# One accumulator for the weighted values of a head pair's row group

## The chip, the cores and the metric

The kernel runs on one core of a Trainium2 chip. The metric is device time in microseconds (us), the median of 3 runs: 1600.85 us before the change (1600.73 to 1602.08).

## The reference

Top-32 attention followed by a gated feed-forward layer, in float32:

```python
# q, k, v: batch 8, heads 8, sequence 576, head dim 64
scores = scale * np.matmul(q, k.transpose(0, 1, 3, 2))
kth = np.partition(scores, -32, axis=-1)[..., -32:-31]
scores = np.where(scores >= kth, scores, -1e9)
attn = np.exp(scores - np.max(scores, axis=-1, keepdims=True))
attn = attn / (np.sum(attn, axis=-1, keepdims=True) + 1e-09)
attn_out = np.matmul(attn, v)
# x: 4608 tokens x 512
gate = 1.0 / (1.0 + np.exp(-(x @ w_gate)))
out = (gate * (x @ w_val)) @ w_out          # 512 -> 1536 -> 512
```

## The kernel before, in words

Attention goes by steps. A step is one row tile `i` (128 queries; the fifth, `i == 4`, has the remaining 64) of one pair of heads `p` (four pairs) of one batch. The steps are sorted by row groups: the list `groups` holds (batch, first tile, end). Batch 0 has the groups 0-1, 2-3 and 4; odd batches have 0-1 and 2-4; even batches have 0-2 and 3-4. Within a group all row tiles of one pair come first, then those of the next pair.

For a step, `scores` forms the products of queries and keys (L191) and ScalarE (ACT) copies them out; `select` finds the threshold of each row, mostly on VectorE (DVE: L256, L260, L284) with ACT and GpSimd (POOL) beside it (L268, L274); `masked` applies the mask (DVE, L210) and spreads each row's inverse sum over a tile `inv` (POOL, L216).

Two steps later `turn` transposes the masked tile on TensorE (PE, L296, L301), three or four 128-column pieces to one PSUM tile of the ring `ps_t`, which has two tiles, and ACT copies each to `et` (L297). A buffer `et` takes the transposes of two full row tiles (256 columns), or of one (128), or of the last (64).

Then `weigh` runs once for each `et`, 108 times in all. Both heads of a pair stand in one product's 128 output rows, head A in the lower 64 and head B in the upper 64. Keys come in chunks of 128; each head has four chunks of its own, whose values fill only half of PE's columns. Their products are the half-column products (L315 for the upper half, L316 for the lower; a pair of them runs side by side). The fifth chunk is shared by the heads and is a full product, the mixed one (L317). In a 64-column block all chunks are half-column products (L320, L321), and the last two use only 64 rows of PE (L322, L323). Behind them the inverses are transposed into the other half of the same PSUM tile (L326), ACT copies these to `rs` (L329), DVE multiplies (L332, L336), and each piece is split into a rounded and a remaining part, `xh` (ACT, L339) and `xl` (POOL, L340), which the feed-forward layer reads.

`ffn` works on units of 256 or 384 tokens: the two first products as three partial products each (L368 to L370), the gate on ACT, DVE and POOL, the last product likewise (L387 to L389). Its steps are mixed among the attention's steps by the table `MILES`. During the first attention steps `split_weights` reads the weights and splits each in two parts: DVE writes a `lead` and a `frac` tile (L133 to L138), PE forms the rest from them (L140 to L142), ACT copies it out (L143).

The order of instructions on each engine is not that of the source: a scheduler sets it from data dependences, buffers and priorities. Each engine runs its own order strictly.

## Time and profile before

| | before |
|---|---|
| median of 3 runs | 1600.85 us |
| profiled execution | 1602.43 us |
| its span, first to last instruction | 1600.5 us |
| granted TensorE clock, mean | 0.988 |
| PE busy | 1534.2 us |
| DVE busy | 1317.3 us |
| ACT busy | 1127.3 us |
| POOL busy | 1097.4 us |

The profiled execution took 1.9 us more than its span. "PEld" is the weight loads of PE, which overlap its products. A busy share is a mean over the span. The ends of products on PE are modelled, so that their durations overlap: the time that PE takes for one is read from its start to the next start.

### The profile page before, as it was taken

To read this page: it belongs to the slowest core of one execution; us is meant where nothing else is said; L and a number is where in the kernel's file an instruction comes from. 1 tells how busy PE (TensorE), PEld (TensorE's weight loads), DVE (VectorE), ACT (ScalarE), POOL (GpSimd) and SP (SyncE) were. 2 spreads that over 40 slices of the span, in tenths; PEclk is the share of its full clock that TensorE was granted. 3 is DMA by queue.
4 is the path that set the end of the run, shared out by engine and by line. 5 is a ranking of instruction groups with operands and counts; after the bars stand their busy time and mean duration, and the time that the engine had idled before them with its cause. 6 is when DMAs were issued, how large, how long until landed. Compare 5 with 4: busy or idle time off the path is not lost.

```text
span 1600.5 us, 34265 instructions
## 1 busy us (share of the span) xinstructions
PE 1534.2 (96%) x10586; PEld 1397.7 (87%) x10586; DVE 1317.3 (82%) x5895; ACT 1127.3 (70%) x2531; POOL 1097.4 (69%) x1799
## 2 busy tenths in 40 slices
PE   5769889999999999999999999999999999999998
PEld 3437669999989999988999999999999999999998
DVE  7999997888998878898988788888988888888201
ACT  7778876778777777778677778768777778667221
POOL 7556876688776786688767786678766887665111
PEclk8889999999999999999999999999999999999999
DMA  7664788786755665655555575566555665564574
GB/s 268 206 204 153 235 278 320 275 300 240 272 185 181 233 225 188 201 200 194 203 200 190 214 250 191 191 235 216 192 201 180 225 229 194 195 207 170 178 283 160
DMA packets 92065, 346.65 MB, mean 217 GB/s; under 512 B 10208, under 2 KB 37344, under 8 KB 63456
## 3 DMA queue, kind: packets, MB, share of 16 engines
q1 hardware_dynamic: 91872, 344.37, 61.8%
q8 instruction: 86, 1.41, 0.4%
q14 instruction: 107, 0.88, 0.2%
HBM read 316.01 MB, written 28.31 MB: 215 GB/s over the span
## 4 chain that ended last, share of the span: by engine, by line
PE 82%; DVE 10%; DMA 3%; POOL 2%; ACT 2%; issue 1%; SPq 0%; POOLq 0%; ACTq 0%; DVEq 0%
PE pz L369 12%; PE pz L370 12%; PE pz L368 12%; PE pss L191 9%; PE pt L296 6%; PE po L315 6%; PE po L387 6%; PE po L388 6%; PE po L389 6%; PE po L317 2%; DMA wraw<-in_w_dram 2%; DVE cand L256 2%; DVE e L210 2%; PE po L326 1%; DVE kths L284 1%
## 5 line engine op out<-in xcount | busy, mean ns | idle before, releaser
L274 POOL TENSOR_TENSOR u<-s,under 128x288 f32<-128x288 f32 x576 | 457.6, 816 | 116.7 <-ACT under L268 105.2
L256 DVE MAX8 cand<-s 128x8 f32<-128x72 f32 x2304 | 349.4, 219 | 60.4 <-ACT s L198 59.3
L368 PE MATMUL pz<-xh,w 128*128 128x384 f32 (+1 forms) x1184 | 393.0, 333 | 0.2 <-ACT gf L373 0.2
L369 PE MATMUL pz<-xl,w 128*128 128x384 f32 (+1 forms) x1184 | 388.3, 328 | 1.5 <-POOL xl L340 1.5
L370 PE MATMUL pz<-xh,w 128*128 128x384 f32 (+1 forms) x1184 | 388.6, 328 | 0.0
L210 DVE SCALAR_TENSOR_TENSOR e<-s,kths,e 128x576 f32<-128x576 f32 x288 | 280.3, 979 | 5.7 <-ACT e L205 5.6
L268 ACT ACTIVATE under<-s,leads 128x576 bf16<-128x576 f32 x288 | 223.0, 775 | 77.2 <-DVE leads L260 38.8
L284 DVE MAX8 kths<-u 128x8 f32<-128x584 f32 x288 | 219.2, 761 | 41.4 <-POOL u L275 40.0
L376 POOL TENSOR_TENSOR gl<-gf,gh 128x384 fp32r<-128x384 f32 (+1 forms) x156 | 153.6, 986 | 120.7 <-ACT gh L375 116.2
L205 ACT ACTIVATE e<-s,st 128x576 f32<-128x576 f32 x288 | 209.6, 772 | 28.4 <-POOL st L264 28.0
L369 PEld LDWEIGHTS pz<-xl,w 128*128 128x128 f32 x1184 | 223.4, 189 | 2.0 <-POOL xl L340 2.0
L368 PEld LDWEIGHTS pz<-xh,w 128*128 128x128 f32 x1184 | 223.1, 189 | 1.0 <-ACT gf L373 0.4
L370 PEld LDWEIGHTS pz<-xh,w 128*128 128x128 f32 x1184 | 223.1, 189 | 0.0
L191 PE MATMUL pss<-k,qh 128*128 128x288 f32 (+2 forms) x672 | 196.2, 310 | 25.1 <-ACT s L198 18.3
L198 ACT ACTIVATE s<-pss 128x576 f32<-128x576 f32 x288 | 184.9, 642 | 41.3 <-PE pss L191 37.7
L297 ACT ACTIVATE et<-pt 128x384 f32<-128x384 f32 x384 | 178.5, 488 | 37.3 <-PE pt L296 36.5
L296 PE MATMUL pt<-ident,e 128*128 128x128 f32 x1152 | 181.7, 277 | 15.1 <-DVE e L210 11.1
L388 PE MATMUL po<-gl,w 128*128 128x384 f32 (+1 forms) x592 | 194.5, 331 | 0.7 <-POOL gl L376 0.7
L389 PE MATMUL po<-gh,w 128*128 128x384 f32 (+1 forms) x592 | 192.9, 328 | 0.0
L387 PE MATMUL po<-gh,w 128*128 128x384 f32 (+1 forms) x592 | 191.4, 337 | 0.0
L191 PE MATMUL pss<-k,ql 128*128 128x288 f32 (+2 forms) x672 | 184.4, 296 | 0.0
L296 PEld LDWEIGHTS pt<-ident,e 128*128 128x128 f32 x1152 | 142.8, 142 | 30.8 <-DVE e L210 16.4
(97 smaller groups left out, 3240.0 us busy)
## 6 DMA issues: line engine op xcount, KB each, us to landing
w<-ws SPq DMA_DIRECT2D x222, 1024.0 KB, 5.0
v<-in_v_dram SPq DMA_DIRECT2D x68, 352.0 KB, 3.6
qraw<-in_q_dram SPq DMA_DIRECT2D x160, 128.0 KB, 3.3
kraw<-in_k_dram SPq DMA_DIRECT2D x64, 288.0 KB, 3.2
wraw<-in_w_dram SPq DMA_DIRECT2D x36, 512.0 KB, 4.7
ws<-w_split SPq DMA_DIRECT2D x36, 512.0 KB, 4.4
out_dram<-acc SPq DMA_DIRECT2D x40, 192.0 KB, 5.2
out_dram<-acc SPq DMA_DIRECT2D x12, 128.0 KB, 4.7
```

Of the source, the lines that this page charges most:

```text
L191: nc.tensor.matmul(ps[:, half, o : o + n], x[:, h * P : (h + 1) * P], ks[h][:, k0 : k0 + n], start=t == 0, stop=t == len(todo) - 1,)
L210: nc.vector.scalar_tensor_tensor(e[:, j], s[:, j], kth[j], e[:, j], op0=ALU.is_ge, op1=ALU.mult, accum_out=st[:, 4 + j : 5 + j])
L256: nc.vector.max(cand[:, j, 8 * g : 8 * g + 8], s[:, j, g * SEG : (g + 1) * SEG])
L274: nc.gpsimd.tensor_tensor(u[:, j, part], s[:, j, part], under[:, j, part], op=ALU.mult)
L284: nc.vector.max(kths[:, n_tiles - col - j : n_tiles - col - j + 8], u[:, j])
L296: nc.tensor.transpose(pt[:, c], ef[:, k0 : k0 + P], ident)
L368: nc.tensor.matmul(ps, wt[:, u, 0, d], xh, start=d == 0, stop=False)
L369: nc.tensor.matmul(ps, wt[:, u, 0, d], xl, start=False, stop=False)
L370: nc.tensor.matmul(ps, wt[:, u, 1, d], xh, start=False, stop=d == NP - 1)
L387: nc.tensor.matmul(ps, wt[:, e % 2, 0, f], gh, start=f == 0, stop=False)
L388: nc.tensor.matmul(ps, wt[:, e % 2, 0, f], gl, start=False, stop=False)
L389: nc.tensor.matmul(ps, wt[:, e % 2, 1, f], gh, start=False, stop=f == FG - 1)
```

## The change

`weigh` is called once for each pair and row group, with all its blocks, and forms them side by side in the columns of one PSUM tile: 68 calls in the place of 108. Of the 40 merged calls 16 have a 256- and a 64-column block, 12 a 256- and a 128-column block, 12 a 128- and a 64-column block.

The last block comes first. Where it has 128 columns its mixed product is formed before its half-column products. The half-column products of the next block are chained to the last one of the block before, and the mixed product of the first block comes at the end. All these products get a raised priority for the scheduler. Three inverses and up to 384 columns no longer fit one PSUM bank; then the inverses go to a tile `rb` of the transposes' ring. ACT copies all inverses of a call at once.

A buffer pool `spare` is opened when the weights are split. From then on every third `et` comes from it, so there are three; it also holds `rs` with 384 columns and the `inv` tiles, four in the place of three. The `frac` tiles of the split go from three to two.

```diff
-                    frac = parts.tile([P, NP * P], F32R, tag="frac", name=f"wt_frac_{idx}_{i}")
+                    frac = parts.tile([P, NP * P], F32R, tag="frac", bufs=2, name=f"wt_frac_{idx}_{i}")
...
+        pools["spare"] = ctx.enter_context(tc.tile_pool(name="late", bufs=1, reuse_waits="tile"))
...
-        inv = bi.tile([P, P], F32, tag="inv", name=f"inv_{nm}")
+        inv = (pools["spare"] if "spare" in pools else bi).tile([P, P], F32, tag="inv", bufs=4 if "spare" in pools else 3, name=f"inv_{nm}")
...
-    def weigh(et, vt, n, invs, pieces, nm):
+    def weigh(blocks, vt, pieces, nm):
+        n = sum(cols for _, cols, _ in blocks)
+        m = sum(len(invs) for _, _, invs in blocks) * P
+        po = ps_o.tile([P, 4 * P], F32, tag="o", name=f"po_{nm}")
+        rb = po[:, 4 * P - m :]
+        if n + m > 4 * P:
+            rb = ps_t.tile([P, 4, P], F32, tag="t", name=f"rb_{nm}").rearrange("p a n -> p (a n)")[:, :m]
+        mixed = vt[:, 4:6].rearrange("p a d -> p (a d)")
+        at = [sum(cols for _, cols, _ in blocks[:x]) for x in range(len(blocks))]
+        last = None
+        for x in reversed(range(len(blocks))):
+            et, cols, _ = blocks[x]
+            top = po[:, at[x] : at[x] + cols]
+            early = x > 0 and cols > REM
+            with ExitStack() as queued:
+                queued.enter_context(tc.high_priority(offset=RAISE))
+                if early:
+                    nc.tensor.matmul(top, mixed, et[:, 4, :cols], start=True, stop=False)
+                if last is not None:
+                    queued.enter_context(tc.issue_after(last.ins))
+                if cols > REM:
+                    for c in reversed(range(4)):
+                        for d, v0, e0 in ((slice(D, P), 6, 5), (slice(0, D), 0, 0)):
+                            last = nc.tensor.matmul(
+                                top[d],
+                                vt[:, v0 + c],
+                                et[:, e0 + c, :cols],
+                                start=c == 3 and not early,
+                                stop=c == 0 and early,
+                            )
+                else:
+                    for c in range(4):
+                        nc.tensor.matmul(top[:D], vt[:, c], et[:, c, :REM], start=c == 0, stop=False)
+                        nc.tensor.matmul(top[D:], vt[:, 6 + c], et[:, c, REM:P], start=c == 0, stop=False)
+                    nc.tensor.matmul(top[:D], vt[:REM, 4], et[:REM, 4, :REM], start=False, stop=True)
+                    last = nc.tensor.matmul(top[D:], vt[:REM, 10], et[:REM, 4, REM:P], start=False, stop=True)
+                if cols > REM and not early:
+                    nc.tensor.matmul(top, mixed, et[:, 4, :cols], start=False, stop=True)
+        for t, inv in enumerate(inv for _, _, invs in blocks for inv in invs):
+            nc.tensor.transpose(rb[:, t * P : (t + 1) * P], inv, ident)
...
+        nc.scalar.activation(rs[:, :m], rb, AF.Copy)
...
-                et, o, invs = b2.tile([P, 9, 2 * P], F32, tag="et", name=f"et_{nm}"), 0, []
+                pool = pools["spare"] if "spare" in pools and turns % 3 == 2 else b2
+                et, o, invs = pool.tile([P, 9, 2 * P], F32, tag="et", name=f"et_{nm}"), 0, []
+                turns += 1
...
             if len(invs) == 2 or i >= end - 1 or i == NT - 1:
+                blocks.append((et, o, invs))
+            if i == end - 1:
...
-                weigh(et, values[g, p], o, invs, pieces, nm)
+                weigh(blocks, values[g, p], pieces, nm)
+                blocks = []
```

In the pieces of the engines' orders below, line numbers are those of the version shown: after the change the half-column products are L333 (128 rows) and L342 to L345 (64-column block), the early mixed product L327, the late one L347, the transposed inverses L350, the feed-forward products L395 to L397 and L414 to L416. `po` is the accumulator, `v` the values, `pss` scores, `pz` feed-forward sums.

On PE in batch 4, pair 3, group 0-2, before: the block of row tiles 0 and 1.

```order
L368 MATMUL pz_2_1_1_13885<-xh_1_9957,w_9_13868 128x384
L315 MATMUL po_1_3_13761<-et_0_3_13614,v_3_13491 64x256
L316 MATMUL po_1_3_13761<-et_0_3_13614,v_3_13491 64x256
...
L317 MATMUL po_1_3_13761<-et_0_3_13614,v_3_13491 128x256
L326 MATMUL po_1_3_13761<-ident,inv_0_3_13422 128x128
L326 MATMUL po_1_3_13761<-ident,inv_1_3_13561 128x128
L191 MATMUL pss_4_1_0_13787<-k_1_2_11999,qh_4_1_13495 128x288
```

The block of row tile 2 follows later as a run of its own, in the same form with 128 columns. After the change, the same group:

```order
L414 MATMUL po_6_2_1_14189<-gh_2_2_13924,w_16_14063 128x384
L327 MATMUL po_2_3_13825<-et_2_3_13807,v_3_13414 128x128
L350 MATMUL rb_2_3_13826<-ident,inv_0_3_13330 128x128
...
L414 MATMUL po_6_2_1_14189<-gh_2_3_14030,w_16_14063 128x384
L333 MATMUL po_2_3_13825<-et_2_3_13807,v_3_13414 64x128 x8
L333 MATMUL po_2_3_13825<-et_0_3_13537,v_3_13414 64x256 x8
L347 MATMUL po_2_3_13825<-et_0_3_13537,v_3_13414 128x256
L193 MATMUL pss_4_1_0_13691<-k_1_2_11921,qh_4_1_13418 128x288
```

The half-column products of both blocks stand in one run, and the mixed product of the smaller block and the inverses stand ahead, among feed-forward products.

On PE at a 64-column block, batch 5, pair 2, before:

```order
L296 MATMUL pt_2_3_0_17521<-ident,e_2_3_17162 128x128
L320 MATMUL po_4_2_17417<-et_4_2_17407,v_2_17033 64x64
L321 MATMUL po_4_2_17417<-et_4_2_17407,v_2_17033 64x64
...
L322 MATMUL po_4_2_17417<-et_4_2_17407,v_2_17033 64x64
L323 MATMUL po_4_2_17417<-et_4_2_17407,v_2_17033 64x64
L326 MATMUL po_4_2_17417<-ident,inv_4_2_17205 128x128
L296 MATMUL pt_2_3_1_17526<-ident,e_2_3_17162 128x128 x3
```

After, the same row group:

```order
L342 MATMUL po_4_2_17291<-et_4_2_17281,v_2_16924 64x64
L343 MATMUL po_4_2_17291<-et_4_2_17281,v_2_16924 64x64
L350 MATMUL rb_4_2_17292<-ident,inv_2_2_16831 128x128
...
L193 MATMUL pss_0_0_1_17173<-k_0_1_17156,ql_0_0_16929 128x288
L344 MATMUL po_4_2_17291<-et_4_2_17281,v_2_16924 64x64
L345 MATMUL po_4_2_17291<-et_4_2_17281,v_2_16924 64x64
L333 MATMUL po_4_2_17291<-et_2_2_17014,v_2_16924 64x256 x8
L347 MATMUL po_4_2_17291<-et_2_2_17014,v_2_16924 128x256
```

The 64-row pair stands directly ahead of the other block's products; here other work lies between it and its own block's first eight products. In 15 of the 28 such calls the whole run is unbroken, in 12 it is split in this way.

On DVE at the end of the weights' split, before (`wt_frac` is the fraction tile, `cand` the segments' maxima of a row tile's scores):

```order
L256 MAX cand_0_0_3328<-s_0_0_3104 128x8 x7
L137 TENSOR_SCALAR wraw_1_2638<-wt_lead_1_2640 128x512
L138 SCALAR_TENSOR_TENSOR wt_frac_0_2625<-wraw_0_2622 128x512
L262 MATCH_REPLACE cand_4_3_3200<-tops_4_3_3201,cand_4_3_3200 128x64
L260 MAX tops_0_0_3329<-cand_0_0_3328 128x8
L393 SCALAR_TENSOR_TENSOR acc_1_0_1731<-po_0_2_0_2593,acc_1_0_1731 128x256
L332 TENSOR_TENSOR rs_3_3_3079<-po_3_3_3067,rs_3_3_3079 128x256
L138 SCALAR_TENSOR_TENSOR wt_frac_1_2641<-wraw_1_2638 128x512
```

After:

```order
L139 SCALAR_TENSOR_TENSOR wt_frac_0_2625<-wraw_0_2622 128x512
L258 MAX cand_1_0_3466<-s_1_0_3190 128x8 x5
L135 SCALAR_TENSOR_TENSOR wt_lead_1_2640<-wraw_1_2638,wt_lead_1_2640 128x512
L258 MAX cand_1_0_3466<-s_1_0_3190 128x8 x11
L286 MAX kths<-u_4_3_3208 128x8
L138 TENSOR_SCALAR wraw_1_2638<-wt_lead_1_2640 128x512
L420 SCALAR_TENSOR_TENSOR acc_1_1_1746<-po_0_2_1_2607,acc_1_1_1746 128x256
L139 SCALAR_TENSOR_TENSOR wt_frac_1_2641<-wraw_1_2638 128x512
```

The last fraction now stands behind the sixteen segment maxima of a further row tile and one long maximum.

## Rows read from the trace of the kernel before

**Rows 1.** The page: busy times with shares of the span; the chain's shares.

```profile
PE 1534.2 (96%) x10586; PEld 1397.7 (87%) x10586; DVE 1317.3 (82%) x5895; ACT 1127.3 (70%) x2531; POOL 1097.4 (69%) x1799
...
PE 82%; DVE 10%; DMA 3%; POOL 2%; ACT 2%; issue 1%; SPq 0%; POOLq 0%; ACTq 0%; DVEq 0%
```

**Rows 2.** Stages: from:to, length, busy us of PE, PEld, DVE, ACT, POOL; clock; DMA.

```profile
0.00:134.00 134.00, 88.46 (x366) 54.02 (x367) 121.44 (x494) 102.37 (x208) 82.93 (x127) 0.88 0.68 224
134.00:240.00 106.00, 95.70 (x614) 75.23 (x613) 104.66 (x392) 86.02 (x191) 82.64 (x115) 0.97 0.67 225
240.00:1560.00 1320.00, 1315.02 (x9413) 1234.30 (x9412) 1084.33 (x4997) 934.34 (x2125) 926.73 (x1553) 1.00 0.62 217
```

**Rows 3.** Waits of PE after 240 us: us in total, times, longest us.

```profile
PE pt L296 <- ACT et L297: 1.7, 3, 1.0
...
PE pz L368 <- ACT gf L373: 0.2, 1, 0.2
```

**Rows 4.** Timeline of PE, 256-column block: start us, us, instruction.

```profile
806.30 0.29 PE L191 MATMUL pss<-k,qh 128*128 128x288 f32 x1
806.43 0.29 PE L191 MATMUL pss<-k,ql 128*128 128x288 f32 x1
806.65 0.43 PE L315 MATMUL po<-et,v 128*64 128x256 f32 x1
...
806.92 0.38 PE L315 MATMUL po<-et,v 128*64 128x256 f32 x1
...
807.13 0.38 PE L315 MATMUL po<-et,v 128*64 128x256 f32 x1
...
808.21 0.38 PE L315 MATMUL po<-et,v 128*64 128x256 f32 x1
...
808.53 0.70 PE L317 MATMUL po<-et,v 128*128 128x256 f32 x2
809.06 0.38 PE L326 MATMUL po<-ident,inv 128*128 128x128 f32 x2
```

**Rows 5.** Timeline of PE, the end of a 64-column block.

```profile
922.73 0.22 PE L320 MATMUL po<-et,v 128*64 128x64 f32 x1
...
922.78 0.22 PE L320 MATMUL po<-et,v 128*64 128x64 f32 x1
...
922.94 0.27 PE L322 MATMUL po<-et,v 64*64 64x64 f32 x1
...
923.05 0.22 PE L322 MATMUL po<-et,v 64*64 64x64 f32 x1
...
923.21 0.33 PE L326 MATMUL po<-ident,inv 128*128 128x128 f32 x1
```

**Rows 6.** Groups by line: busy us, mean ns | idle before, its releasers.

```profile
L317 PEld LDWEIGHTS po<-et,v 128*128 128x128 f32 x152 | 22.8, 188 | 22.4 <-issue 22.4
...
L297 ACT ACTIVATE et<-pt 128x384 f32<-128x384 f32 x384 | 178.5, 488 | 37.3 <-PE pt L296 36.5
...
L256 DVE MAX8 cand<-s 128x8 f32<-128x72 f32 x2304 | 349.4, 219 | 60.4 <-ACT s L198 59.3
...
L284 DVE MAX8 kths<-u 128x8 f32<-128x584 f32 x288 | 219.2, 761 | 41.4 <-POOL u L275 40.0
...
L216 POOL COPY inv<-st 128x128 f32<-128x128 f32 x160 | 56.5, 356 | 63.7 <-DVE st L214 30.4 <-PE po L326 14.1 <-DVE tops L260 11.0
```

**Rows 7.** Timeline of DVE and PE: fractions of the weights written and read.

```profile
134.77 1.10 DVE L138 SCALAR_TENSOR_TENSOR wt_frac<-wraw 128x512 fp32r<-128x512 uint32 x1
142.86 0.67 DVE L138 SCALAR_TENSOR_TENSOR wt_frac<-wraw 128x512 fp32r<-128x512 uint32 x1
...
150.15 0.39 PE L142 MATMUL wrest<-wt_frac,plus 128*128 128x512 f32 x1
...
228.97 0.67 DVE L138 SCALAR_TENSOR_TENSOR wt_frac<-wraw 128x512 fp32r<-128x512 uint32 x1
...
232.63 0.50 PE L142 MATMUL wrest<-wt_frac,plus 128*128 128x512 f32 x1
```

More of the change, by code (lines that the diff above doesn't have):

```diff
@@ L66, in tile_topk_attention_then_gated_ffn @@
     SOON, RUSH = 8, 15
+    RAISE = 200
     HELD = 2 * (2 * FG + NE // 2)
@@ L305, in turn @@
             nc.scalar.activation(et[:REM, 4, :P], pt[:REM, 0], AF.Copy)
-    def weigh(et, vt, n, invs, pieces, nm):
-        both = ps_o.tile([P, 4 * P], F32, tag="o", name=f"po_{nm}")
-        po, rb = both[:, :n], both[:, 2 * P :]
-        if n > REM:
-            mixed = vt[:, 4:6].rearrange("p a d -> p (a d)")
-            for c in reversed(range(4)):
-                nc.tensor.matmul(po[D:], vt[:, 6 + c], et[:, 5 + c, :n], start=c == 3, stop=False)
-                nc.tensor.matmul(po[:D], vt[:, c], et[:, c, :n], start=c == 3, stop=False)
-            nc.tensor.matmul(po, mixed, et[:, 4, :n], start=False, stop=True)
-        else:
-            for c in range(4):
-                nc.tensor.matmul(po[:D], vt[:, c], et[:, c, :REM], start=c == 0, stop=False)
-                nc.tensor.matmul(po[D:], vt[:, 6 + c], et[:, c, REM:P], start=c == 0, stop=False)
-            nc.tensor.matmul(po[:D], vt[:REM, 4], et[:REM, 4, :REM], start=False, stop=True)
-            nc.tensor.matmul(po[D:], vt[:REM, 10], et[:REM, 4, REM:P], start=False, stop=True)
-        for t, inv in enumerate(invs):
-            nc.tensor.transpose(rb[:, t * P : (t + 1) * P], inv, ident)
-        rs = b1.tile([P, 2 * P], F32, tag="rs", name=f"rs_{nm}")
-        m = len(invs) * P
-        nc.scalar.activation(rs[:, :m], rb[:, :m], AF.Copy)
-        xf = rs[:, :n]
-        if n > REM:
-            nc.vector.tensor_tensor(xf, po, rs[:, :n], op=ALU.mult)
-        else:
-            for h in range(2):
-                d = slice(h * D, h * D + D)
-                nc.vector.tensor_tensor(xf[d], po[d], rs[d, h * REM : h * REM + REM], op=ALU.mult)
@@ new lines, in weigh @@
+    def weigh(blocks, vt, pieces, nm):
[38 more added lines that the diff above has]
+            nc.tensor.transpose(rb[:, t * P : (t + 1) * P], inv, ident)
+        if "spare" in pools:
+            rs = pools["spare"].tile([P, 3 * P], F32, tag="rs", name=f"rs_{nm}")
+        else:
+            rs = b1.tile([P, 2 * P], F32, tag="rs", name=f"rs_{nm}")
+        nc.scalar.activation(rs[:, :m], rb, AF.Copy)
+        xf = rs[:, :n]
+        for (_, cols, _), o in zip(blocks, at):
+            if cols > REM:
+                nc.vector.tensor_tensor(xf[:, o : o + cols], po[:, o : o + cols], rs[:, o : o + cols], op=ALU.mult)
+            else:
+                for h in range(2):
+                    d, r = slice(h * D, h * D + D), o + h * REM
+                    nc.vector.tensor_tensor(xf[d, o : o + cols], po[d, o : o + cols], rs[d, r : r + cols], op=ALU.mult)
@@ L436, in run @@
         todo, work, at, col, ready = [], 0, 0, 0, 0
-        parts, done = {}, {}
+        parts, done, blocks, turns = {}, {}, [], 0
         taken, lead = 0, 2 * (FG + NE // 2)
@@ L499, in run @@
             if len(invs) == 2 or i >= end - 1 or i == NT - 1:
-                t, left, pieces = b * S + (i + 1 - len(invs)) * P, o, []
+                blocks.append((et, o, invs))
+            if i == end - 1:
+                t, left, pieces = b * S + first * P, sum(cols for _, cols, _ in blocks), []
                 while left:
```

## The prediction

> **What bounds the kernel now.** I read the page first, its busy shares and its chain of waits [rows 1]: TensorE (PE) is busy for 96% of the span and carries 82% of the chain. Then the busy times by stage [rows 2], because that share is a mean over two unlike stretches. Up to 240 us PE is busy 88.46 of 134 us and 95.70 of 106 us, while VectorE (DVE) has 104.66 of the second 106: there DVE sets the pace and PE has 55.8 us idle. From 240 to 1560 us PE is busy 1315.02 of 1320 us. In that stretch the end moves with PE's own work, microsecond for microsecond. Third, what PE waits for after 240 us [rows 3]: its six rows come to 5.2 us, the first of them, 1.7 us, for transposes that want a PSUM tile back from ScalarE (ACT). None of the six is a wait for a DVE mask. So what the change can give must come out of PE's instructions themselves, and the view for that is the timeline of one run of half-column products [rows 4].
>
> A busy PE hides small losses, because a product's end is modelled and overlaps the next start. They are seen between starts. In [rows 4] a 288-column score product is followed by the next 0.13 us later (806.30 to 806.43), but by the first half-column pair 0.22 us later: 0.09 us lost. From the first pair to the second are 0.27 us, between later ones 0.21: 0.05 us more. From the last pair to the mixed product are 0.32 us, 0.10 over a pair. The mixed product runs as two passes; its two and the step to the next operation take 0.53 us where two passes at a pair's rate take 0.43: 0.10 us. The weight loads say so too: the mixed product's loads sat behind 22.4 us of "issue" idle in all [rows 6], waiting for nothing but PE's own state. A 64-column block [rows 5] pays 0.10 us where it goes from its 128-row chunks to its 64-row pair (0.16 between starts, where chunks follow at 0.05 to 0.06), and 0.05 us at its end (0.16 where the pairs follow at 0.11).
>
> **The change, part by part.** The arithmetic stays: the same products, transposes and weight loads, in the same shapes. What goes is borders. Counted over the whole PE order, runs of half-column products begin 122 times before and 83 times after (108 and 68 calls, the rest are runs that other work splits), so there are 39 fewer. The sum on PE:
> - beginnings: 39 x (0.09 + 0.05) = 5.5 us less;
> - ends in 128-row half columns: 90 before, 78 after, 12 x 0.10 = 1.2 us less;
> - ends in a 64-row pair: 32 before, 5 after, 27 x 0.05 = 1.3 us less;
> - the step from 128-row chunks to the pair: 30 before, 20 after (the new order often leaves the pair for later, the second order piece shows it), 1.0 us less;
> - mixed products right behind a run: 71 and 64, 0.7 us less;
> - new: 28 steps from the 64-row pair back to 128-row half columns of another block. No row shows one. From below, a pair's end costs 0.05; from above, beginning a run and its slow first pair cost 0.14. I take 0.10, the price of the opposite step [rows 5]: 2.8 us more (1.4 to 3.9).
>
> That makes 7.0 us less on PE (5.8 to 8.3), nearly all of it after 240 us, because batch 0 merges nothing. The twelve mixed products that now come early stand among full-array work and should cost their two passes and no border.
>
> The Trainium skill, page "TensorEngine Tiling (Array Packing)", section "Tiling Modes", Key Properties, says that changing the tiling mode drains TensorE and that changing only the tile does not. The trace agrees: 0.09 to 0.10 us at changes of mode, none between the two blocks' pairs of one mode. The rule speaks against a part of this change: a 64-column block's pair is a mode of its own, so merging it with a full block adds a change. By the rule alone there are 274 changes before and 214 after, 60 x 0.10 = 6.0 us less.
>
> *The split of the weights (up to 240 us).* The fraction tile goes from three buffers to two, and the first instruction that moves for it is a DVE one. Before, DVE writes a fraction at 134.77 us which PE reads at 150.15, and writes the one two later at 142.86 [rows 7]. With two buffers that write has to come after the read. The order puts it 24 rows later and puts other DVE work in its place, so DVE, the pacemaker, does not stand still; but the pieces of the split shift. The last fraction is written from 228.97 us and read at 232.63, 3.0 us after it is done. In the new order a second row tile's sixteen short maxima (0.219 us each) and one long one (0.761) [rows 6] stand ahead of it: 4.3 us later at the most, of which PE has 3.0 us to spare. With the pieces before it I take 2 us more. Against that PE's feed-forward work stands earlier around there, and of its 10.3 us idle between 134 and 240 us it might fill some. Ends: 3 us less to 5 us more.
>
> *Copies of the inverses, now for 28 calls in a tile of the transposes' ring.* That ring has two tiles. A copy out of it takes about 0.49 us [rows 6]; while the inverses hold a tile, transposes have the other. Waits for that ring are 1.7 us after 240 us. On the whole the order puts the ring's users as far apart as before, with a few more close ones, so I add 0.5 us (1 us less, since a third `et` lets ACT copy earlier, to 4 us more).
>
> *Hidden parts.* Forty fewer copies and forty fewer casts on ACT, forty fewer subtractions on GpSimd (POOL): neither engine sets the pace in [rows 1], and a removal can only help, so nothing. The inverse tiles go from three to four, but three are now held until the end of a row group. POOL already waits 14.1 us in all for PE to read one [rows 6]; behind such a wait stand the products for the next threshold, and the DVE maxima wait for these. PE had no wait for a mask after 240 us, so this slack covers it; if it were used up, the transposes would show it in [rows 3].
>
> Sum: -7.0 + 2 + 0.5 = -4.5 us. The profiled execution took 1602.43 us (span 1600.5 and 1.9 around it), so 1597.9 by its own measure; from the median of the runs, 1600.85, it is 1596.3. Changes within 0.2%, 3.2 us, are what a measurement of this kernel can't tell from none.
>
> **Rivals.**
> 1. *The borders shrink, but the start gives it back.* If the late pieces of the split cost their whole 5 us, or each step out of the 64-row pair costs 0.14 or more and the ring takes its 4 us, between 0 and 3 us remain: 1598 to 1602. For it: DVE has 1.3 us of slack in 106 us, and the moved write is on it. Against: PE has other work standing there. Chance 0.29.
> 2. *The ring of the transposes becomes the bound* (slower). The inverses take one of its two tiles 28 times, and ACT must empty it between its other activations; PE, which runs its queue in order, then stands at a transpose with all products behind it. The longest such wait so far was 1.0 us [rows 3]. At 0.25 us on each of the 28 this eats the whole 7.0 us; at 0.4 us it costs 11.2, which with the start's 2 us is 1607; 1603 to 1608. For it: two tiles, and the merged calls need three transposes at once. Against: ACT is on time now. Chance 0.14.
> 3. *The change does more than its borders.* Queued runs also let the array load the next weights without breaks, and PE's start-up idle is filled: 10 to 13 us less, 1588 to 1591. For it: twelve early mixed products, feed-forward work moved forward. Against: no row shows a loss beyond those summed. Chance 0.15.
>
> **How the numbers follow.** The forecast, 1592 to 1597.6, has 0.42. Faster by over 0.2% is the forecast with the third rival, 0.57; within 0.2% the first with a share of the second's near end, 0.30; slower 0.13. The range goes from 1588 (third rival) to 1604 (the ring at a little over 0.3 us each and the start's 2 us).
>
> **What would show it.** Right: starts in a merged run of 128- and 256-column pairs follow at 0.11 and 0.21 us with no break between blocks; the first pair still comes 0.09 late and only one mixed product shows its 0.10. Against the sizes: the step from the 64-row pair to the next block's chunks is far from 0.10 over a pair. For the first rival: PE is busy for less than 95.7 us between 134 and 240 us. For the second: more than 5 us of PE waits for ACT at transposes after 240 us, and a lower busy time there. The prediction is wrong if the stretch from 240 us to the last masks gets no shorter although the borders are gone.

## The result and the profile after

The change made the kernel slower: 1615.44 us median of 5 runs (1615.12 to 1620.22) against 1601.65 us of the kernel before beside it, a ratio of 1.0101 (95% interval 1.0087 to 1.0115). I had predicted 1596.3 us, with 1604 as the upper end. The profiled execution took 1615.16 us, its span 1613.1 us. Two executions reported further down, one of c_before (1708.66 us) and one of f_inv4 (3373.45 us), were in a slower state, and the medians given for these two runs leave them out.

The page after: busy times, and the chain's shares, which answer to [rows 1].

```profile
PE 1538.8 (95%) x10586; PEld 1410.3 (87%) x10586; DVE 1316.7 (82%) x5895; ACT 1112.2 (69%) x2451; POOL 1081.7 (67%) x1759
...
PE 68%; POOL 2%; DVE 2%; ACT 2%; issue 1%; POOLq 0%; ACTq 0%; DVEq 0%
```

PE is busy 4.6 us longer although nothing was added to it. The shares of the chain can't be set beside those of [rows 1]: they add up to 75% only, because the chain that the page follows back from the end breaks off at 398 us. From there on PE carries about nine tenths of it. The stages of [rows 2], after (from:to, length, busy us of PE, PEld, DVE, ACT, POOL; granted clock; DMA):

```profile
0.00:134.00 134.00, 93.86 (x376) 59.34 (x377) 124.20 (x499) 104.74 (x213) 83.23 (x129) 0.84 0.67 224
134.00:240.00 106.00, 92.46 (x573) 73.36 (x572) 103.72 (x383) 80.51 (x174) 76.06 (x110) 0.95 0.65 213
240.00:1560.00 1320.00, 1305.18 (x9373) 1231.20 (x9373) 1080.23 (x5000) 919.33 (x2050) 914.33 (x1513) 0.99 0.62 215
```

Between 134 and 240 us PE is busy 3.2 us less, after 240 us 9.8 us less. The waits of PE after 240 us (us in total, times, longest) come to 14.1 us, where [rows 3] had 5.2:

```profile
PE pss L193 <- ACT s L200: 4.6, 5, 1.8
PE pt L298 <- DVE e L212: 3.0, 2, 2.0
PE po L414 <- DVE acc L420: 2.8, 3, 1.5
PE pt L298 <- ACT et L299: 1.8, 1, 1.8
```

The largest is one of scores for ACT, which has yet to empty a score tile; the second is the wait for a mask that the kernel before did not have after 240 us.

I set the two traces side by side at equal PE work (the sum of the products' nominal times up to there). Up to 1034 us the version after was 0.2 us late against an execution of the kernel before that began well (c_before, below), after having been 6.6 us late at 368 us: 6.4 us gained in the middle. Then it lost 15.0 us between 1034 and 1075 us, and little anywhere else. The slices there, after, same columns:

```profile
1035.00:1040.00 5.00, 5.00 (x37) 3.92 (x35) 4.57 (x17) 3.04 (x8) 2.74 (x6) 1.00 0.70 280
1040.00:1045.00 5.00, 4.47 (x30) 3.90 (x29) 4.93 (x40) 4.69 (x13) 3.26 (x7) 1.00 0.37 99
1045.00:1050.00 5.00, 2.36 (x18) 1.89 (x16) 5.00 (x24) 4.65 (x11) 4.79 (x8) 1.00 0.11 28
1050.00:1055.00 5.00, 4.31 (x21) 2.73 (x23) 4.35 (x22) 3.77 (x9) 4.68 (x8) 0.79 0.31 87
1055.00:1060.00 5.00, 3.79 (x24) 2.47 (x20) 3.01 (x23) 3.41 (x6) 4.29 (x9) 0.87 0.45 129
1060.00:1065.00 5.00, 2.52 (x12) 2.06 (x13) 4.99 (x31) 5.00 (x15) 4.55 (x10) 0.81 0.15 56
1065.00:1070.00 5.00, 5.00 (x21) 4.90 (x21) 5.00 (x22) 3.93 (x9) 4.60 (x6) 0.50 0.07 8
1070.00:1075.00 5.00, 5.00 (x33) 4.97 (x33) 3.59 (x27) 3.07 (x8) 4.67 (x8) 1.00 0.88 288
```

Read them from the left: PE falls to 2.36 us while DVE and ACT are full; for 30 us the attention chain, not PE, sets the pace. The last columns say why: DMA falls to 8 GB/s, because the weights that feed-forward products stream are not asked for; SyncE issues no transfer of weights between 1033.0 and 1069.9 us. In the trace no feed-forward product starts between 1044.6 and 1066.1 us. What PE waits for between 1036 and 1076 us is mostly ACT, which empties score tiles and transposes late, and only once a mask:

```profile
PE pss L193 <- ACT s L200: 4.4, 4, 1.8
PE pt L298 <- ACT et L299: 1.8, 1, 1.8
PE pt L298 <- DVE e L212: 1.0, 1, 1.0
```

Then read the clock in the slices: it drops after idle stretches (from 1052.9 and from 1063.1 us on), and at 1065 to 1070 us PE is busy for the whole slice at 0.50, that is at 1.2 GHz. Idle PE between 1036 and 1076 us comes to 7.6 us; 10.2 us at the lower clock lose half, 5.1. That is 12.7 of the 15.0 us; 2.3 us I could not assign. The Trainium skill (page "TensorE: Matmul & The Clock Gate", section "Part 1: The HAM clock gate") says that the lower clock is the state at rest and that activity lifts it; the slice of 5.00 busy us at 0.50 agrees, since the lift came only at 1069.9 us.

Why the products are missing can be read in the order. This feed-forward unit is 384 rows, and its products need the weighted values of all four head pairs for these rows. The order has 8.1 us of PE work (an estimate, from the counted products and their durations) without a feed-forward product ahead of the 3484th, the 28th of unit 8, which reads pair 3 of batch 5's first row group. The kernel before has one stretch of 4.6 us after 240 us, at another unit; PE waits 2.0 us there (near 690 us), and its clock stays up.

The stretch had announced itself: from 790 us on the masks were late, and PE covered it with feed-forward products, 24 more by 1040 us than c_before (41 more than the first profile of the kernel before, which stood 3.4 us further back). The masks up to 1040 us and the last of them, before (in the first line each mask counts as two instructions; in the second the times are those of the first and the last start):

```profile
0.00:1040.00 1040.00, 193.60 (x396) 0.98 0.64 223
L210 DVE SCALAR_TENSOR_TENSOR e<-s,kths,e x288: 793/820/1573, 33.7 to 1483.6; 128x576 f32<-128x576 f32 x144
```

and after:

```profile
0.00:1040.00 1040.00, 185.96 (x387) 0.97 0.65 225
L212 DVE SCALAR_TENSOR_TENSOR e<-s,kths,e x288: 790/817/1604, 33.9 to 1507.9; 128x576 f32<-128x576 f32 x144
```

So 198 masks had begun by 1040 us before and 194 after, and at the same count those after stood 28 us later than in c_before. ACT's waits for the threshold between 790 and 1040 us grow too, from 7.0 to 33.9 us, but they alone tell little: a_et2 (below) has 27.3 us of them and loses nothing at this place.

None of this shows on PE until its store of other work is empty. Why the masks slipped there, I did not find out.

### The profile page after: what moved, and what is told of

It reads as the page before. It is cut to its first block, busy times and chain, and to the rows that moved or that the text cites. A ratio compares the mean times of both kernels' runs of the same rounds, so it can differ in the third digit from the quotient of the medians.

```text
span 1613.1 us, 34058 instructions
## 1 busy us (share of the span) xinstructions
PE 1538.8 (95%) x10586; PEld 1410.3 (87%) x10586; DVE 1316.7 (82%) x5895; ACT 1112.2 (69%) x2451; POOL 1081.7 (67%) x1759
## 4 chain that ended last, share of the span: by engine, by line
PE 68%; POOL 2%; DVE 2%; ACT 2%; issue 1%; POOLq 0%; ACTq 0%; DVEq 0%
PE pz L395 10%; PE pz L396 10%; PE pz L397 10%; PE pss L193 7%; PE pt L298 6%; PE po L333 5%; PE po L414 5%; PE po L415 5%; PE po L416 5%; PE po L347 2%; POOL k L161 1%; PE po L342 1%; POOL u L276 1%; PE pt L303 1%; DVE kths L286 1%
## 5 line engine op out<-in xcount | busy, mean ns | idle before, releaser
L395 PE MATMUL pz<-xh,w 128*128 128x384 f32 (+1 forms) x1184 | 392.0, 333 | 0.9 <-ACT gf L400 0.9
L397 PE MATMUL pz<-xh,w 128*128 128x384 f32 (+1 forms) x1184 | 389.9, 329 | 0.0
L212 DVE SCALAR_TENSOR_TENSOR e<-s,kths,e 128x576 f32<-128x576 f32 x288 | 275.3, 959 | 5.2 <-ACT e L207 3.5
L286 DVE MAX8 kths<-u 128x8 f32<-128x584 f32 x288 | 219.1, 761 | 47.3 <-POOL u L277 45.3
L395 PEld LDWEIGHTS pz<-xh,w 128*128 128x128 f32 x1184 | 223.4, 189 | 2.0 <-ACT gf L400 1.2
L397 PEld LDWEIGHTS pz<-xh,w 128*128 128x128 f32 x1184 | 223.9, 189 | 0.3
L414 PE MATMUL po<-gh,w 128*128 128x384 f32 (+1 forms) x592 | 190.6, 337 | 3.3 <-DVE acc L420 2.8
L416 PE MATMUL po<-gh,w 128*128 128x384 f32 (+1 forms) x592 | 192.1, 328 | 0.0
L193 PE MATMUL pss<-k,ql 128*128 128x288 f32 (+2 forms) x672 | 188.4, 301 | 0.0
```

Of the source, the lines that this page charges most:

```text
L193: nc.tensor.matmul(ps[:, half, o : o + n], x[:, h * P : (h + 1) * P], ks[h][:, k0 : k0 + n], start=t == 0, stop=t == len(todo) - 1,)
L212: nc.vector.scalar_tensor_tensor(e[:, j], s[:, j], kth[j], e[:, j], op0=ALU.is_ge, op1=ALU.mult, accum_out=st[:, 4 + j : 5 + j])
L286: nc.vector.max(kths[:, n_tiles - col - j : n_tiles - col - j + 8], u[:, j])
L395: nc.tensor.matmul(ps, wt[:, u, 0, d], xh, start=d == 0, stop=False)
L397: nc.tensor.matmul(ps, wt[:, u, 1, d], xh, start=False, stop=d == NP - 1)
L414: nc.tensor.matmul(ps, wt[:, e % 2, 0, f], gh, start=f == 0, stop=False)
```

## The experiments

**Theory 1** says: the borders give what was predicted or more, and feed-forward work running dry at a unit border takes it back, by idle PE and then by its clock. **Rival A** blames the third `et` tile itself, **rival B** the start (two fraction tiles), as my first rival had it. Two numbers of PE's order serve as forecasts: its changes of tiling mode (274 before, 214 after) and its stretches of 4 us or more without a feed-forward product. To compare traces I split PE's time from its first to its last start into idle time, time at the lower clock (L, of which half is lost) and the rest, the work at full clock:

| | time, median | changes | span of starts | idle | L | work |
|---|---|---|---|---|---|---|
| before | 1600.85 | 274 | 1588.7 | 60.8 | 29.7 | 1513.0 |
| before again (c_before) | 1600.66 | 274 | 1585.0 | 54.1 | 37.7 | 1512.1 |
| after | 1615.44 | 214 | 1601.2 | 68.5 | 57.6 | 1503.9 |
| a_raise0 | 1611.88 | 319 | 1598.9 | 56.5 | 47.3 | 1518.8 |
| a_et2 | 1599.91 | 222 | 1584.4 | 58.4 | 43.7 | 1504.1 |
| c_frac | 1612.59 | 208 | 1600.4 | 72.1 | 49.0 | 1503.8 |
| d_first50 | 1592.49 | 178 | 1577.7 | 55.5 | 50.4 | 1497.0 |
| g_start | 1589.17 | 190 | 1576.0 | 55.7 | 41.4 | 1499.7 |
| f_frac2 | 1615.57 | 286 | 1600.4 | 61.3 | 52.5 | 1512.9 |

**No raised priority (a_raise0).**

```diff
-    RAISE = 200
+    RAISE = 0
```

> The changed kernel with the raised priority at zero; merging, the queued run, the inverses in the transposes' ring, three et buffers and two fraction tiles stay. In the changed kernel's order PE has a stretch of attention work alone of some 8 us of its own work, behind the 27th product of the feed-forward unit that follows batch 5's first row group; here the longest such stretch is 4.7 us, at batch 3. Theory 1 (PE runs out of feed-forward work at that unit's border, waits for the attention chain there and loses its clock): the 15 us between 1034 and 1075 us go, 1594 to 1601 us. Theory 2 (the inverses in the transposes' ring make PE wait, my second rival): nothing of that is undone, 1611 to 1618 us. Theory 3 (the split of the weights with two fraction tiles costs it): 1611 to 1618 us as well.

1611.88 us, ratio 1.0069 (1.0053 to 1.0086): far above what theory 1 said, and in the range of theories 2 and 3. The time alone would speak for them; the trace does not. PE waits only 1.2 us after 240 us and is busy at full clock from 1034 to 1075 us, so the dry stretch is gone, although the inverses' ring and the fraction tiles are those of the version after; but without priority the runs are broken up: 319 changes and 14.9 us more work than after. The experiment exchanged one cost for another; what it tells is the borders' price, 14.9 us for 105 changes.

**Two `et` tiles (a_et2).**

```diff
-                pool = pools["spare"] if "spare" in pools and turns % 3 == 2 else b2
+                pool = b2
```

> The changed kernel with two et buffers in the place of three; all else of the change stays, the raised priority too. No stretch of attention work alone over 4 us is in its PE order. Theory 1: 1593 to 1600 us, no stall over 5 us after 240 us. Theories 2 and 3: 1611 to 1618 us, or more, since ACT has one buffer less to copy into.

1599.91 us, 0.9992 (0.9982 to 1.0001): the loss at this border is gone, and the version is as fast as the kernel before. PE's row between 1036 and 1076 us:

```profile
1036.00:1076.00 40.00, 39.89 (x275) 36.81 (x274) 34.97 (x159) 29.57 (x64) 33.43 (x52) 1.00 0.67 235
```

Alone this does not tell theory 1 from rival A, since the order lost its dry stretch with the tile.

**The kernel before, paced to run dry (b_dry), and with priority alone (b_raise).** The first changes the pacing table, so that feed-forward work is asked for earlier; the second raises the priority of the half-column and mixed products by 200.

```diff
-    MILES = [(512, 256), (832, 512), (1152, 768), (1536, 1152), (1984, 1536)]
+    MILES = [(512, 256), (832, 512), (1152, 768), (1536, 1152), (1984, 1664)]
```

> The kernel before, without any merging, with the feed-forward work let 128 tokens closer to the attention (the last entry of the table that paces it 1664 in the place of 1536). Its PE order has eight stretches of attention work alone of 4 to 8.4 us of work at unit borders, where the kernel before has one of 4.6. Theory 1: PE waits at these, with granted clock down, and it takes 1625 to 1680 us. Theories 2 and 3: nothing that they speak of is in it, 1598 to 1606 us.

1635.1 us, 1.0213 (1.0193 to 1.0234): with eight stretches of 4 to 8.4 us and nothing of the change in it, it is 34 us slower. PE's waits after 240 us are led by the same line as after, scores for ACT (8.1 us). About 9 us of its loss appear as work in my split and are not explained.

```diff
-            for c in reversed(range(4)):
+            with tc.high_priority(offset=200):
+                for c in reversed(range(4)):
...
-            for c in range(4):
+            with tc.high_priority(offset=200):
+                for c in range(4):
...
```

> The kernel before with the raised priority for its half-column and mixed products, 108 calls as they were. Theory 1: its order has no stretch longer than the 4.6 us that the kernel before has too, so 1598 to 1605 us. If the raised priority in itself holds attention up: 1608 to 1618 us.

1601.35 us, 1.0004 (0.9994 to 1.0014): priority alone takes 20 changes away and does not move the time. In its split 3.5 us of work are gone against c_before, while idle time is 1.3 us more and the lower clock takes 2.2 us more.

**Three fraction tiles on top of two `et` tiles (c_frac).**

```diff
-                    frac = parts.tile([P, NP * P], F32R, tag="frac", bufs=2, name=f"wt_frac_{idx}_{i}")
+                    frac = parts.tile([P, NP * P], F32R, tag="frac", name=f"wt_frac_{idx}_{i}")
```

> The changed kernel with two `et` tiles as before and also three fraction tiles as before. Its TensorE order once more holds a stretch without any feed-forward product, 7.1 us of TensorE work at the same border (before product 3484) where the changed kernel has 8.1 us; the version with two `et` tiles alone has none. Theory 1 (what costs the time is feed-forward work running dry at that border, whatever tile count led there): 1606 to 1613 us, TensorE waits for ACT and DVE near 1040 to 1065 us and a granted clock under 0.9 in a 5 us slice there. Rival A (the third `et` tile itself holds things up): like the version with two `et` tiles, 1597 to 1602 us. Rival B (the two fraction tiles cost the start its time): better than that version, 1593 to 1598 us, with TensorE busy 95 us or more between 134 and 240 us where it had 92.9.

1612.59 us, 1.0073 (1.0058 to 1.0087). This run decides: there is no third `et`, and the order that came out has its stretch of 7.1 us at the same border, and 10 us are lost there.

```profile
1036.00:1076.00 40.00, 33.88 (x207) 28.96 (x206) 35.25 (x189) 30.48 (x70) 30.43 (x52) 0.91 0.45 150
```

Rival A falls, and rival B as the main cause. Which tile counts an order has does not say whether it runs dry; the order itself does.

**Attention asked for earlier (c_lag).** The version after, with more distance in the pacing table.

```diff
-    MILES = [(512, 256), (832, 512), (1152, 768), (1536, 1152), (1984, 1536)]
+    MILES = [(512, 256), (832, 512), (1152, 768), (1536, 1152), (1984, 1472)]
```

> The changed kernel with all its tile counts, and in the last entry of the pacing table 1472 in place of 1536, so that attention work is asked for a little earlier against the feed-forward products. Its order has three short stretches without feed-forward products, 4.6, 4.4 and 4.0 us of TensorE work, in place of the 8.1 (the kernel before has one of 4.6). Theory 1: most of the loss at 1040 to 1075 us goes, 1599 to 1606 us. Rival A (the third `et` tile): the loss stays, 1611 to 1617 us. Rival B (the start): it stays as well, 1611 to 1617 us.

1607.2 us, 1.0043 (1.0029 to 1.0058): 8 us come back, a little less than I expected. Of the 15 us only 1 to 2 are left at 1036 to 1076 us, with all tiles of the change in place. The masks are as late as after (194 begun by 1040 us), so it is the missing store of feed-forward products that makes their lateness cost time. That the total gains less has its place before the border: at 1034 us c_lag is 6.2 us behind c_before, where the version after was 0.2.

```profile
1036.00:1076.00 40.00, 38.94 (x254) 36.63 (x251) 34.90 (x177) 31.45 (x69) 30.74 (x52) 1.00 0.59 203
```

**A lower priority (c_raise50)**, two `et` tiles and RAISE = 50:

> The changed kernel with two `et` tiles and a raised priority of 50 in place of 200: the order has no stretch of 4 us or more without feed-forward products, and about as few changes of mode as with 200. Theory 1: 1597 to 1602 us, as with 200; if fewer entries to runs count, 1 us less. Rival A: the same. A rival that the high priority draws attention forward too far: 1592 to 1597 us.

1602.8 us, 1.0014 (1.0005 to 1.0022), a miss by a little: no stretch, and in its trace 3.6 us of waits for feed-forward sums on ACT and 3.4 us at the lower clock near 1086 us. An order without stretches is not thereby free of waits.

**The kernel before once more (c_before).**

> The kernel before, unchanged, profiled once more, for the start alone. If the low clock of the first 240 us is a matter of the single execution: granted clock 0.83 to 0.86 and TensorE busy 92 to 94 us in the first 134 us, as in the versions profiled so far, against 88.5 us in the first profile, and a span up to 7 us other than 1600.5. If it belongs to the order of the kernel: 88 to 89 us again.

1600.66 us, its profiled execution 1598.83. The order is the same, yet the start is not (compare [rows 2]):

```profile
0.00:134.00 134.00, 95.84 (x380) 59.77 (x381) 123.55 (x498) 104.67 (x214) 83.70 (x129) 0.85 0.68 224
134.00:240.00 106.00, 94.96 (x633) 75.41 (x632) 104.88 (x398) 85.55 (x190) 83.50 (x119) 0.98 0.70 234
```

PE's busy time at the start was higher in the execution that was granted less clock (95.84 us at 0.85, 88.46 at 0.88). Yet at the work that it reaches at 341 us this one is 3.4 us ahead of the first profile: it idles 6.7 us less, which is more than the lower clock costs it. From there to the end that lead changes by 0.2 us at most. So a difference under some 4 us at the start says nothing from one profile; later on one of 1 us may.

**The 64-row pair first (d_first400, d_first, d_first50).** With two `et` tiles. In a 64-column block the pair goes ahead of the chunks, so that chunks lead directly to the next block; priorities of 400, 200 and 50.

```diff
+                    nc.tensor.matmul(top[:D], vt[:REM, 4], et[:REM, 4, :REM], start=True, stop=False)
+                    nc.tensor.matmul(top[D:], vt[:REM, 10], et[:REM, 4, REM:P], start=True, stop=False)
                     for c in range(4):
-                        nc.tensor.matmul(top[:D], vt[:, c], et[:, c, :REM], start=c == 0, stop=False)
-                        nc.tensor.matmul(top[D:], vt[:, 6 + c], et[:, c, REM:P], start=c == 0, stop=False)
-                    nc.tensor.matmul(top[:D], vt[:REM, 4], et[:REM, 4, :REM], start=False, stop=True)
-                    last = nc.tensor.matmul(top[D:], vt[:REM, 10], et[:REM, 4, REM:P], start=False, stop=True)
+                        nc.tensor.matmul(top[:D], vt[:, c], et[:, c, :REM], start=False, stop=c == 3)
+                        last = nc.tensor.matmul(top[D:], vt[:, 6 + c], et[:, c, REM:P], start=False, stop=c == 3)
```

> The changed kernel with two `et` tiles, a raised priority of 400, and in a 64-column block the 64-row pair ahead of its chunks, so that the step from the pair back to the next block's chunks is gone. Changes of TensorE's mode in the order: 168, against 222 of the version with two `et` tiles alone and 274 of the kernel before; no stretch of 4 us without feed-forward products. Theory 1 (time is the borders' price, 0.13 to 0.15 us for each change, plus what the feed-forward work running dry costs): 54 x 0.13 to 0.15 is 7 to 8 us off that version's 1599.9, so 1591 to 1594 us, and no drop of the clock at 1040 to 1075 us. A rival by which changes of mode are free and only long waits count: 1598 to 1602 us. A rival by which the higher priority draws attention work forward and costs elsewhere: 1600 us or more.

1595.32 us, 0.9971 (0.9960 to 0.9982), a miss by 1.3 us: against a_et2 the work is 8.5 us less, as the changes said, but PE idles 6.1 us more, which the count of stretches does not show.

> The same with the raised priority of 200: 176 changes of mode, hardly more, but the order holds stretches without feed-forward products of 8.1 us at the border before product 3484, of 7.1 before 4780 and of 4.6 and 4.1. Theory 1: the borders' gain is lost again, 1606 to 1616 us, with TensorE idle and its clock lower near 1040 to 1075 us and again near 1370 to 1400 us. A rival by which only borders count: 1592 to 1595 us, as with 400.

1610.41 us, 1.0059 (1.0044 to 1.0075).

> The same with a raised priority of 50: 178 changes of mode, one stretch of 4.4 us without feed-forward products before product 2188, where the kernel before has 4.6 us and loses nothing. Theory 1: 1592 to 1596 us. A rival by which a low priority splits the runs and costs time: 1600 us or more.

1592.49 us, 0.9953 (0.9939 to 0.9966).

The three differ by at most ten changes of mode, and d_first and d_first50 by two; 18 us lie between those two, of which 10 arise at the first border and 5 at the second. c_raise50 differs from d_first50 in the place of the pair alone: 1.0014 against 0.9953. The rows of d_first at both borders (I had placed the second one 25 us too early):

```profile
1036.00:1076.00 40.00, 34.35 (x202) 30.90 (x201) 35.98 (x192) 31.78 (x71) 34.03 (x57) 0.91 0.51 174
1400.00:1430.00 30.00, 27.65 (x177) 24.86 (x174) 28.52 (x151) 24.60 (x55) 19.29 (x37) 0.94 0.52 177
```

and that of d_first50 at the first:

```profile
1036.00:1076.00 40.00, 40.00 (x276) 36.91 (x275) 33.82 (x165) 28.90 (x65) 32.28 (x53) 1.00 0.63 228
```

**The start (e_start, f_frac2, f_inv4, g_start).** All versions with the change that have been shown so far reach the work of 341 us 5 to 8 us later than c_before, where the first profile of the kernel before, b_raise and b_dry are 1.1 to 3.4 us late. e_start is d_first50 with batch 1 not merged; f_frac2 and f_inv4 are the kernel before with two fraction tiles, and with four inverse tiles in a pool of their own; g_start is e_start with three fraction tiles.

```diff
-            if i == end - 1:
+            if blocks and (i == end - 1 or b < 2):
...
```

> The fastest version so far (two `et` tiles, raised priority of 50, the 64-row pair first), with the blocks of batch 1 weighed one by one again, as in the kernel before; merging begins with batch 2. Changes of mode: 186 against 178 (1.1 us more at 0.14 each); the longest stretch without feed-forward products stays 4.4 us. It asks where the start's 4 to 5 us went (TensorE reaches the same work at 341 us in the kernel before and 5 to 8 us later in all versions with merged blocks). Theory M (merged blocks put off the weighted values of batch 1, which were the work that filled TensorE's waits there): TensorE busy 94 to 96 us between 134 and 240 us, the fraction waits under 1.5 us, and the time 1589 to 1592 us. Rival T (tile counts: two fraction tiles, four inverse tiles): busy 92 to 93 us again with fraction waits of 3 us or more, and the time 1592 to 1595 us.

1593.1 us, 0.9952 (0.9938 to 0.9966), 6.8 us late: theory M, that merging alone does it, falls.

```diff
-                    frac = parts.tile([P, NP * P], F32R, tag="frac", name=f"wt_frac_{idx}_{i}")
+                    frac = parts.tile([P, NP * P], F32R, tag="frac", bufs=2, name=f"wt_frac_{idx}_{i}")
```

> The kernel before with two fraction tiles in place of three, and nothing else of the change. Its order has 286 changes of mode in place of 274, so 1.7 us more at 0.14 each. My step (the split of the weights costs 2 us, between 3 us less and 5 more): 1604 to 1606 us with fraction waits of TensorE of 2 us or more between 134 and 240 us, against 0.5 before. If the two tiles are the whole loss of the start (4 to 5 us): 1606 to 1609 us. If they cost nothing: 1601.5 to 1603.5 us and no fraction waits.

1615.57 us, 1.0099 (1.0085 to 1.0114), far more than any case had: 8.7 us late at 341 us, and six more lost in small pieces further on, which I did not trace one by one. Against c_before its split shows 7.2 us more idle time and 14.8 us more at the lower clock, but only 0.8 us more work. By itself this is as much as the whole change lost; but a_et2 has two fraction tiles as well and takes 1599.91 us, so they do not make up the loss of the version after. Nor does the count of stretches foretell this run: after 240 us its longest is that of the kernel before.

```diff
+        pools["spare"] = ctx.enter_context(tc.tile_pool(name="late", bufs=1, reuse_waits="tile"))
...
-        inv = bi.tile([P, P], F32, tag="inv", name=f"inv_{nm}")
+        inv = (pools["spare"] if "spare" in pools else bi).tile([P, P], F32, tag="inv", bufs=4 if "spare" in pools else 3, name=f"inv_{nm}")
```

> The kernel before with four inverse tiles in a pool of their own, laid out after the weights' split has ended, and nothing else of the change. Changes of mode: 289, so 2.1 us more at 0.14 each; the first row in which VectorE's order differs is the 496th, at about 240 us. If the inverse tiles are the loss of the start: 1606 to 1609 us, and TensorE 4 us or more late at the work that it reaches at 341 us. If they cost nothing there: 1602 to 1604 us.

1602.78 us, 1.0010 (1.0002 to 1.0019), 3.7 us late, as the kernel before can be: no cost of the inverse tiles at the start is to be seen.

> The version in which merging begins with batch 2 (two `et` tiles, raised priority of 50, the 64-row pair first), now with three fraction tiles as well, so that nothing of the change is left in the first 220 us. Changes of mode 190, against 186 with two fraction tiles and 178 of the version that merges batch 1 (0.6 and 1.7 us more at 0.14 each); the longest stretch without feed-forward products 4.4 us. If two fraction tiles and merged blocks in batch 1 are each enough by themselves to lose the start's 4 to 5 us: TensorE as early as in the kernel before at the work that it reaches at 341 us (0 to 4 us late in place of 6 to 7), fraction waits between 134 and 240 us under 1.5 us, and 1588 to 1591 us. If another part of the change is behind it: 6 to 7 us late again, 1593 to 1596 us.

1589.17 us, 0.9925 (0.9911 to 0.9938), 3.8 us late. The waits of PE for a fraction between 134 and 240 us, in c_frac (three tiles, batch 1 merged):

```profile
PE wrest L143 <- DVE wt_frac L139: 3.3, 3, 2.6
```

in e_start (two tiles, not merged):

```profile
PE wrest L143 <- DVE wt_frac L139: 2.9, 2, 1.7
```

in f_frac2 (two tiles, nothing merged at all):

```profile
PE wrest L142 <- DVE wt_frac L138: 2.5, 2, 1.7
```

and in g_start (three tiles, not merged):

```profile
PE wrest L143 <- DVE wt_frac L139: 0.8, 2, 0.6
```

Two fraction tiles are enough for the loss of the start (f_frac2). Merged blocks in batch 1 seem to be enough too (c_frac), which is less firmly shown, since c_frac differs from g_start in priority and in the place of the pair as well. With neither the loss is gone: by one profile g_start is 3.0 us less late than e_start, and by the medians 3.9 us faster. g_start is the fastest version, 0.75% under the kernel before: it keeps the merged runs, puts the pair first, and leaves the start alone. Its stages and longest waits after 240 us:

```profile
134.00:240.00 106.00, 96.46 (x588) 76.66 (x589) 105.29 (x396) 83.57 (x181) 78.34 (x112) 0.94 0.66 221
240.00:1560.00 1320.00, 1316.57 (x9504) 1245.86 (x9503) 1090.08 (x4998) 927.13 (x2064) 925.66 (x1520) 1.00 0.63 219
```

```profile
PE po L414 <- DVE acc L420: 1.5, 2, 1.3
PE po L414 <- ACT acc L418: 0.5, 1, 0.5
```

## Why the prediction was wrong

*The borders: right in mechanism, a little small.* I had 7.0 us (5.8 to 8.3; the terms listed add up to 6.9). The work at full clock fell from 1512.1 to 1513.0 to 1503.9 us, 8.2 to 9.1 us, for 60 changes. Over 16 profiles (all but b_dry) the work follows the number of changes in a straight line of 0.140 us a change (95% interval 0.126 to 0.153), with no profile more than 2.1 us off it; 60 of them are 8.4 us. The first sign that I had named held too: in a merged run at 1192.56 us the last 128-column pair starts at 1193.38 us and the first two 256-column pairs at 1193.48 and 1193.70, without a break between the blocks. The step from the 64-row pair to the next block, after (timeline of PE: start, us, instruction):

```profile
1083.58 0.22 PE L342 MATMUL po<-et,v 128*64 128x64 f32 x1
...
1083.74 0.27 PE L344 MATMUL po<-et,v 64*64 64x64 f32 x1
...
1083.85 0.22 PE L344 MATMUL po<-et,v 64*64 64x64 f32 x1
...
1084.00 1.52 PE L333 MATMUL po<-et,v 128*64 128x256 f32 x12
```

From the last 64-row pair to the next block are 0.15 us, and then the first 256-column pair takes 0.26 us where later ones take 0.21. What the step costs depends on the pace that one gives the 64-row pairs. By the 0.11 between the two of them, as in my prediction, it is 0.04, and 0.09 with the slow first pair, close to the 0.10 I took. But that 0.11 follows a slow first pair as well; by the 0.05 to 0.06 of the 128-row pairs of that size it is 0.10, and 0.15 in all. Two pairs are too few to tell. The rule of the Trainium skill that I weighed (page "TensorEngine Tiling (Array Packing)", section "Tiling Modes", Key Properties: a change of mode drains TensorE) agrees with these rows. By counted changes at 0.10 it gave 6.0 us; by the 0.140 of the runs it would have given 8.4.

*The start: the right term, its size open.* I took 2 us and gave 5 as the far end. My sign for the first rival came true: PE is busy 92.46 us between 134 and 240 us, less than 95.7. At the work of 341 us the delay is 2.3 or 5.7 us, by which profile of the kernel before one compares with; e_start and g_start, which differ in the fraction tiles alone, lie 3.9 us apart, and PE waits 3.4 us for fractions where it had waited 0.5:

```profile
PE wrest L143 <- DVE wt_frac L139: 3.4, 3, 1.7
```

I had reasoned that the last fraction has 3.0 us to spare. But the waits are three, of up to 1.7 us. And two tiles are not the only way to them (c_frac).

*The transposes' ring: no bound.* After 240 us transposes waited for ACT once, 1.8 us, inside the dry stretch, and no transposed inverse waited for its copy. The second rival had the right sign and the wrong mechanism.

*The hidden parts: the step that failed.* I put them at nothing, for two reasons: ACT and POOL do not set the pace, and "PE had no wait for a mask after 240 us, so this slack covers it." I took the absence of a wait for slack without asking what hid the masks' lateness and how much of it was left. The path that I had named for it did not open: POOL's waits for PE to read an inverse fell from 14.1 us to 5.2, in all of the trace after:

```profile
POOL inv L218 <- PE po L350: 2.7, 2, 2.0
POOL inv L218 <- PE rb L350: 2.5, 2, 2.1
```

The masks came late all the same, the last of them by 24.3 us, so that what I had named as proof against me, a stretch from 240 us to the last masks that gets no shorter, came true. What hides such lateness is a store of feed-forward products, and that store ends at each unit border, where the next products need the weighted values of the row group at hand. There the attention chain sets the pace, ACT and POOL with it. The price is not the delay itself: around that border PE idles 7.6 us, 6.2 of them in waits for ACT and 1.0 for a mask, runs 10.2 us at half speed, and 15 us are lost, nearly twice what all borders of runs gave. That the store ran dry is shown; which part of the change made the masks late stays open. I had compared the two orders run by run and ring by ring, and never counted how much PE work stood between one feed-forward product and the next: 4.6 us at most before, 8.1 after (both after 240 us). That count, to be had before any run, told c_frac, d_first and d_first50 apart. It did not foretell c_raise50 and f_frac2, so it finds this kind of loss and not every one.

Without the dry stretch alone my forecast would still have failed: a_et2, at 1599.91 us, lies where the first rival had put the time, not between 1592 and 1597.6. Without the loss of the start as well the price of the borders is seen nearly whole: g_start, which also puts the pair first, has a lower priority and merges from batch 2 on, has 84 changes fewer than the kernel before, 11.8 us at 0.140, and is 11.2 us faster than the 1600.39 us measured beside it.

## What to carry to other kernels

Where one engine's busy share is near 100% because other work fills its gaps, ask what happens when the filling runs out: find the border at which the filler depends on the very chain that is late, and count in the new order how long the engine goes without filler. Reordering that saves a tenth of a microsecond at each of many places can lose all of it at one such border. And try neighbouring orders (a priority, a pacing constant) before a change is judged: here they moved the same products by 18 us.

## What the runs showed of the hardware that was not expected

- In the slice in which PE was busy for 2.52 of 5 us the clock fell (at 1063.1 us), and it stayed at 1.2 GHz for 6.8 us although PE was busy throughout from 1065 us on: here the engine paid for an idle stretch after it had ended.
- The same program, executed twice, was granted 0.88 and 0.85 of full clock over its first 134 us and stood 3.4 us apart at 341 us, the one with the lower clock ahead; from there to the end the distance changed by 0.2 us at most.
- A change of tiling mode costs 0.140 us all told, by the line through 16 profiles with 168 to 319 of them; single rows show part of it at the change itself and 0.05 us in the slow first pair behind it. No version hid it.
